# Backward chain of a recurrent-memory attention layer: the left queries' part of the key gradient packed by row and head, its rows in three scratch tensors, another issue order

## The chip, the cores and the metric

The kernel runs on one core of one Trainium2 chip. The metric is the device time of one execution in microseconds. A core has TensorE (PE; its weight loads are shown as PEld), VectorE (DVE), ScalarE (ACT), GpSimd (POOL), SyncE (SP), and sixteen DMA engines that SP and POOL issue to.

## The reference, cut to what matters

The forward function normalises x [2048, 512], adds a recurrent attention (A) and a dense layer with squared ReLU (B); what must be computed is its output and the gradients of all ten inputs. The attention runs over 64 segments of 32 rows, one after the other, each with 8 memory rows that come from the segment before:

```python
for s in range(n_seg):
    xs = x[:, s * seg_len:(s + 1) * seg_len, :].copy()
    h = jnp.concatenate([mem, xs], axis=1)             # 8 + 32 rows
    q = jnp.einsum('btd,dhe->bhte', h, Wq)             # 32 heads of 128; k and v alike
    ...
    scores = jnp.where(mask[None, None], scores, -1000000000.0)
    p = _softmax(scores, axis=-1)
    o = jnp.einsum('bhqk,bhke->bhqe', p, v)
    o = jnp.einsum('bhte,hed->btd', o, Wo)
    mem = o[:, :M, :].copy()
    outs.append(o[:, M:, :])
...
_out, _vjp = jax.vjp(_f, A_x, A_mem0, A_Wq, A_Wk, A_Wv, A_Wo, B_w1, B_b1, B_w2, B_b2)
_grads = _vjp(grad_out)
```

The gradient with respect to the memory rows of a segment is needed by the segment before, so the backward pass is a chain of 64 steps too. This case's change is in the gradient with respect to the keys: for each head, the transposed gradient of the scores times the queries, summed over all 40 query rows of a segment.

## The kernel before

The program has five stages: the dense layer and its gradient (to about 290 us); the forward chain (to 1155 us); the left stage, the part of the backward pass that does not depend on the chain (to 1384 us); the backward chain (1384 to about 2318 us); and the weight gradients of the attention (to the end).

**Rows.** The 40 rows of a segment are split. The 32 rows "memory and 24 tokens" are the main rows; the remaining 8 rows of each of four segments are gathered to 32 "left" rows of a block. A block b is four segments (SPB = 4), there are NB = 16 blocks. The 32 heads are four groups (HG = 4) of eight (KH = 8); the group g takes partitions 32g to 32g+31, so one array pass serves four groups side by side. KK is 4, M is 8, L is 40, KW is 64, GW is 1024 (eight heads of 128).

**Left queries in the chain.** A step's key gradient has two parts: from the main queries qN (32 rows) and their score gradients gS, and from the left queries qNL (32 rows of the block, of which 8 belong to the step) and their score gradients GL, which the left stage has computed and stored in S_GSL. In kp (half p of the heads, four heads each) both parts go through outer, which issues for each of four heads and each part four products, one per row group: 16 products from qN with 40 columns and 16 from qNL with 16 columns, which add to the same PSUM:

```python
def kp(p=p):
    outer(pp(p), p, ((KW, L, False, 32, C["qN"], lambda k: gS[:, k, 0:L]),
                     (KW, KW, True, 32, B_["qNL"], pair)))
```

The products from qNL contract all 32 left rows of the block with the columns of GL that belong to the step.

**Scratch.** Left query, key and value rows are computed in the forward part, evicted (L401 and E_ of the forward chain) and stored in one tensor S_NL with three places per row. turned_rows and left_of_step read them back.

**Order.** In the backward chain nothing is planned at run time: B_ORDER lists the operations of four steps, one string for each of the four steps of a block, and play calls them in that order; each engine keeps its own instructions in the order of the calls, and waits for others by semaphores. A name with four plus signs belongs to the step that starts in this string; "L." marks work of a block. The names used here:

- o0mm, o1mm: projection of the output gradient (ps_proj); o0fl, o1fl, o0te, o1te: its transposes and their copies
- vp, kp, qp with half 0 or 1: outer products for v, k and q gradients (b_pp), into one pair of PSUM double banks that all share; ve, vl, ke, kl, qe: their evictions on ACT and DVE, to gv, gk, gq and to b_gvL and b_gkL
- s, d1 to d4, tu: score gradients on TensorE and DVE, and their transposition
- vg, kg, qg: products with the weights (ps_gR, ps_R); ra, rb, ta, tb, Ha, Hb: sum, transposition and reduction to the gradient that the next step starts from
- ldp, ldq, ldn, ldk, vtr, pb, vc: loads of a step and their copies; ldk loads kLs, four loads of 8 rows
- L.G0 to L.I3: left products of the block before (ps_RL); L.vo, L.ko, L.qo (two each): stores of the block's gradients to S_GB; L.lq: the load of gqL; L.ldk: GL and qNL of the next block, on POOL's queue; L.vtr, ktr, qtr and vst, kst, qst: transposes of left gradients and their stores to S_GL

gv, gk and gq have one buffer each, so a block's first evictions wait for the stores of the block before. The loads of qNL, GL, kLs, qN, kN have one buffer, P has two. SP issues the loads of ldk and vtr, all stores and the transposes; POOL issues ldp, ldq, ldn and L.ldv.

## Time and profile before

| what | value |
|---|---|
| median of 3 runs (lowest, highest) | 2909.87 us (2907.95, 2930.09) |
| the profiled execution, its own time | 2896.93 us |
| its span on the core | 2894.9 us |
| granted TensorE clock, mean | 0.978 |
| PE, PEld, DVE, ACT, POOL busy | 94%, 51%, 45%, 36%, 23% |
| DMA: bytes, mean rate | 561.55 MB, 194 GB/s |
| packets under 512 B, of 792984 | 583601 |

Busy time of an engine is the union of its instructions' spans; a matmul's span includes its way through the array, so several products in four row groups overlap. The chain that ended last is 79% on PE and 9% on DMA by the page.

### The profile page before, as it was taken

To read this page: it belongs to the slowest core of one execution; us is meant where nothing else is said; L and a number is where in the kernel's file an instruction comes from. 1 tells how busy PE (TensorE), PEld (TensorE's weight loads), DVE (VectorE), ACT (ScalarE), POOL (GpSimd) and SP (SyncE) were. 2 spreads that over 40 slices of the span, in tenths; PEclk is the share of its full clock that TensorE was granted. 3 is DMA by queue.
4 is the path that set the end of the run, shared out by engine and by line. 5 is a ranking of instruction groups with operands and counts; after the bars stand their busy time and mean duration, and the time that the engine had idled before them with its cause. 6 is when DMAs were issued, how large, how long until landed. Compare 5 with 4: busy or idle time off the path is not lost.

```text
span 2894.9 us, 116348 instructions
## 1 busy us (share of the span) xinstructions
PE 2713.6 (94%) x51700; PEld 1472.0 (51%) x51700; DVE 1298.9 (45%) x3786; ACT 1029.3 (36%) x2362; POOL 658.1 (23%) x1279
## 2 busy tenths in 40 slices
PE   7998899999999888889899999999999889999999
PEld 3554555555555555547455545554555434444444
DVE  5552566666666555444445544554555401100000
ACT  2422445444445444433333333333333301111111
POOL 1000000000000000113333433343344333322221
PEclk9999999999999999999999999999999999999999
DMA  9649377776776666998666787778677799999992
GB/s 262 225 122 239 97 183 189 184 187 182 193 184 179 169 166 161 258 249 247 162 166 173 186 216 177 178 194 208 174 185 193 231 270 221 204 209 248 205 213 68
DMA packets 792984, 561.55 MB, mean 194 GB/s; under 512 B 583601, under 2 KB 683458, under 8 KB 789154
## 3 DMA queue, kind: packets, MB, share of 16 engines
q1 hardware_dynamic: 751426, 430.34, 63.5%
q0 software_dynamic: 41056, 123.77, 14.0%
q8 instruction: 405, 6.64, 0.9%
q14 instruction: 97, 0.79, 0.1%
HBM read 189.15 MB, written 234.11 MB: 146 GB/s over the span
## 4 chain that ended last, share of the span: by engine, by line
PE 79%; DMA 9%; DVE 5%; SPq 3%; issue 3%; ACT 2%; POOL 0%; ACTq 0%; DVEq 0%; POOLq 0%
PE ps_gw L1643 16%; PE ps_proj L428 15%; PE ps_gR L496 11%; PE ps_R L496 5%; PE b_pp L626 3%; PE ps_tr L165 3%; PE ps_L L388 3%; PE ps_RL L1255 3%; DMA b_kLs<-S_NL 2%; PE ps_w L1110 2%; PE ps_sc L473 2%; PE f_pp L626 2%; PE ps_B L340 2%; PE f_T L531 2%; PE b_T L531 2%
## 5 line engine op out<-in xcount | busy, mean ns | idle before, releaser
L1643 PE MATMUL ps_gw<-gn,HNc 128*128 128x512 bf16 x1920 | 418.7, 380 | 2.1 <-DMA gn<-S_GL 2.1
L1643 PEld LDWEIGHTS <-HNc 128*128 128x128 bf16 x1920 | 188.2, 98 | 227.3 <-issue 5.0
L410 ACT CAST f_N<-ps_proj 128x512 bf16<-128x512 f32 x320 | 183.6, 580 | 197.7 <-PE ps_proj L428 189.9
L1576 ACT CAST wt<-ps_gw 128x512 bf16<-128x512 f32 x128 | 74.1, 587 | 454.1 <-PE ps_gw L1643 413.9
L428 PEld LDWEIGHTS <-X 128*32 128x32 bf16 x6144 | 154.3, 96 | 143.6 <-DVE X L540 22.2
L1559 DVE TENSOR_TENSOR gx<-ps_rows,gb 128x512 f32<-128x512 f32 x16 | 11.1, 692 | 431.9 <-PE ps_rows L1557 431.9
L901 POOL COPY kM<-f_kT 128x256 bf16<-128x256 bf16 x64 | 25.6, 401 | 736.7 <-DVE f_kT L413 562.7
L1643 PE MATMUL ps_gw<-GOc,gn 128*128 128x512 bf16 x640 | 141.6, 384 | 8.4 <-ACT wt L1576 6.9
L496 PE MATMUL ps_gR<-Wv,gv 128*32 128x512 bf16 x2048 | 144.5, 403 | 2.5 <-issue 2.3
L496 PE MATMUL ps_gR<-Wk,gk 128*32 128x512 bf16 (+1 forms) x2048 | 139.3, 387 | 1.9 <-issue 0.9
L428 PE MATMUL ps_proj<-Wq,X 128*32 128x512 bf16 x2048 | 134.9, 380 | 2.2 <-issue 2.1
L410 ACT CAST gk<-b_pp 128x256 bf16<-128x256 f32 x192 | 70.7, 379 | 178.4 <-PE b_pp L626 114.2
L496 PE MATMUL ps_R<-Wo,OT 128*32 128x256 bf16 x4096 | 132.9, 286 | 1.1 <-DVE OT L413 1.1
L428 PE MATMUL ps_proj<-Wk,X 128*32 128x512 bf16 x2048 | 132.7, 383 | 0.6
L410 ACT CAST gON<-ps_proj 128x512 bf16<-128x512 f32 x128 | 74.9, 585 | 156.5 <-PE ps_proj L428 156.5
L428 PE MATMUL ps_proj<-Wv,X 128*32 128x512 bf16 x2048 | 129.5, 378 | 0.0
L428 PE MATMUL ps_proj<-Wo,GT 128*32 128x512 bf16 x2048 | 123.7, 382 | 4.2 <-DVE GT L1300 3.5
L1577 POOL DMA_DIRECT2D out_dram<-wt x120 | 64.8, 542 | 268.6 <-ACT wt L1576 253.5
L496 PE MATMUL ps_gR<-Wq,gq 128*32 128x512 bf16 (+1 forms) x2048 | 118.2, 343 | 1.6 <-issue 1.5
L1336 POOL COPY PD<-b_P 32x320 bf16<-32x320 bf16 x256 | 114.7, 448 | 8.0
L496 PEld LDWEIGHTS <-OT 128*32 128x32 bf16 x4096 | 108.1, 101 | 9.2 <-DVE OT L413 1.3
L1331 POOL DMA_DIRECT2D b_P<-S_A x63 | 33.8, 537 | 343.0 <-DVE gS L585 105.0
(283 smaller groups left out, 5346.0 us busy)
## 6 DMA issues: line engine op xcount, KB each, us to landing
S_A<-f_N SPq DMA_DIRECT2D x64, 512.0 KB
out_dram<-wt POOLq DMA_DIRECT2D x134, 128.0 KB, 5.2
S_A<-f_N SPq DMA_DIRECT2D x64, 256.0 KB
S_GB<-gv SPq DMA_DIRECT2D x32, 512.0 KB
S_GB<-gq SPq DMA_DIRECT2D x32, 512.0 KB
S_GB<-gk SPq DMA_DIRECT2D x32, 512.0 KB
b_kN<-S_A POOLq DMA_DIRECT2D x63, 256.0 KB, 3.8
b_qN<-S_A POOLq DMA_DIRECT2D x63, 256.0 KB, 3.8
```

The lines of the kernel that those rows point to most:

```text
L165: nc.tensor.transpose(ps_ap, in_ap, ident[base:base + k, base:base + k])
L388: nc.tensor.matmul(ps[:], lhsT=x(dc), rhs=Wqkv[t][:, dc, c0:c0 + 512], start=(dc == 0), stop=(dc == DC - 1))
L410: nc.scalar.copy(out, in_)
L428: nc.tensor.matmul(o, lhsT=hT[:, dc, :], rhs=x, start=(dc == 0), stop=(dc == DC - 1), tile_position=(0, 32 * g))
L496: nc.tensor.matmul(R[32 * g:32 * g + 32, 0:(cs.stop - cs.start) * P].rearrange("p (a b) -> p a b", b=P), lhsT=XT(k, g), rhs=x[:, cs, :], s ...
L531: nc.tensor.transpose(st["T", h][:, 0, c * P:(c + 1) * P], st["R4"][:, (2 * h + c) * P:(2 * h + c + 1) * P], identF[:])
L626: nc.tensor.matmul(o, lhsT=N_[32 * g:32 * g + m, kk * P:(kk + 1) * P], rhs=X(kk)[32 * g:32 * g + m], start=(i == 0), stop=(i == len(jobs) ...
L1255: nc.tensor.matmul(ps["R", i][32 * g:32 * g + 32, :].rearrange("p (a b) -> p a b", b=P), lhsT=B_[n][:, k, g, :], rhs=W(g * KH + k), start= ...
L1336: nc.gpsimd.tensor_copy(PD[32 * g:32 * g + 32, g], C["P"][32 * g:32 * g + 32, :, 0:L])
L1576: nc.scalar.copy(wt[:], ps[:])
L1577: eng(dst, wt[:])
L1643: nc.tensor.matmul(ps[:], lhsT=l(rc), rhs=r(rc), start=(n == 0), stop=(n == RC_ALL - 1))
```

## The change

The left queries' part of kp becomes four products per half step, one per row group. To that end 8 rows of the step and 4 heads are put on the 32 partitions of a group: qNL is now loaded as [row and head, step, half, 128], and the score gradients are brought to block-diagonal form, so that a partition of one head is zero in the columns of the three others. The left stage sums the score gradients over the steps' places (of which all but one are zero, c0 and c1 on DVE) to gC and stores it in S_GC; ldg loads it by heads, and gx on POOL multiplies it by the one-hot matrix ofk to GX. S_NL becomes three tensors, and the left query rows are stored with the head order changed, for which left_out and the scores of the left rows take care. ldk and the new ldg are four loads each on SP's queue, in place of two on POOL's. LB_ORDER gets c0 and c1, B_ORDER is another order throughout.

The diff, without context where it isn't needed; the calls of outer lose one argument in the other stages, and left_out, the left scores and the loads by S_NL[t] are used alike in the forward part:

```diff
-    S_NL = dram.tile([NB, P, 3, GW], BF16, name="S_NL")
+    S_NL = [dram.tile([NB, P, GW], BF16, name="S_NL%d" % t) for t in range(3)]
-    S_GSL = dram.tile([NB, P, KH, KW], BF16, name="S_GSL")
+    S_GC = dram.tile([NB, P, KK, 4 * M], BF16, name="S_GC")
...
+    ofk = const.tile([P, KK], BF16, name="ofk")
+    with nc.allow_low_precision(reason="all terms of a sum but one are zero"):
+        nc.vector.tensor_reduce(ofk[:], ident[:].rearrange("p (a k) -> p k a", k=KK), axis=AX.X, op=ALU.add)
...
         for dc in range(DC):
             nc.tensor.matmul(ps[:], lhsT=x(dc), rhs=Wqkv[t][:, dc, c0:c0 + 512], start=(dc == 0), stop=(dc == DC - 1))
+    def left_out(cp, dN, ps, t, h):
+
+        if t:
+            cp(dN[:, h * 512:(h + 1) * 512], ps[:])
+        else:
+            cp(dN[:].rearrange("p (k h e) -> p h k e", k=KK, h=2)[:, h], ps[:].rearrange("p (k e) -> p k e", k=KK))
+
     def keep_left(dN, q, t, g):
-        dma(S_NL[4 * q:4 * q + 4, 32 * g:32 * g + 32, t, :].rearrange("b r c -> r b c"), dN[:])
+        dma(S_NL[t][4 * q:4 * q + 4, 32 * g:32 * g + 32, :].rearrange("b r c -> r b c"), dN[:])
     with sb("fl", 2) as fl:
         dma(XL1[:], S_XL[:])
         dma(Wo[:], A_Wo.rearrange("h e d -> e h d"))
...
-                    nc.tensor.matmul(sc3[32 * g:32 * g + 32, k, c:c + n], lhsT=qT[:, 4 * h + k, g, :],
+                    nc.tensor.matmul(sc3[32 * g:32 * g + 32, k, c:c + n], lhsT=qT[:, head(h, k), g, :],
...
         for nm, f in (("mx", mxf), ("sb", sbf), ("ex", exf), ("su", suf), ("rc", rcf), ("pm", pmf)):
             o["%s%d" % (nm, p)] = f
-    def outer(pp, h, jobs, base=0):
+    def outer(pp, h, jobs, base=0, first=True):
         for k in range(4):
-            for i, (c0, w, ends, m, N_, X) in enumerate(jobs):
+            for i, (c0, w, m, N_, X) in enumerate(jobs):
                 for g in range(HG):
                     o = pp[g // 2][:, g % 2, base + k * c0:base + k * c0 + w]
-                    if ends:
-                        o = o.rearrange("p (a n) -> p a n", a=2)[:, :, 0:M]
                     kk = 4 * h + k
                     nc.tensor.matmul(o, lhsT=N_[32 * g:32 * g + m, kk * P:(kk + 1) * P],
-                                     rhs=X(kk)[32 * g:32 * g + m], start=(i == 0), stop=(i == len(jobs) - 1),
+                                     rhs=X(kk)[32 * g:32 * g + m], start=(first and i == 0), stop=(i == len(jobs) - 1),
                                      tile_position=(32 * g, 0), skip_group_check=True)
     def two_of(pp, x, w, base=0, n=4):
...
-                "d10 d20 d30 d40 so- x0- tu0 W0b d11 d21 d31 d41 tu1 v0 x1-").split()
+                "d10 d20 d30 d40 so- x0- tu0 W0b d11 d21 d31 d41 tu1 c0 c1 v0 x1-").split()
...
                     turn(st[p], T["gS"], p)
                 o["tu%d" % p] = tu
+                def own(p=p):
+                    with nc.allow_low_precision(reason="all terms of a sum but one are zero"):
+                        nc.vector.tensor_reduce(
+                            T["gC"][:, :, p].rearrange("p k (a t) -> p k a t", a=2),
+                            T["gS"][:, HALF[p]].rearrange("p k (a j t) -> p k a t j", a=2, j=SPB), axis=AX.X, op=ALU.add)
+                o["c%d" % p] = own
+
                 def qp(p=p):
                     ps["x", p] = [lpp.tile([P, 2, 512], F32, name="l_pp", tag="pp%d" % x) for x in range(2)]
-                    outer(ps["x", p], p, ((32, 32, False, 32, T["kM"], lambda k: st[p][:, k % 4, 0, :]),
-                                          (32, 32, False, 32, T["kL"], lambda k: st[p][:, k % 4, 1, :])))
+                    outer(ps["x", p], p, ((32, 32, 32, T["kM"], lambda k: st[p][:, k % 4, 0, :]),
+                                          (32, 32, 32, T["kL"], lambda k: st[p][:, k % 4, 1, :])))
                 o["qp%d" % p] = qp
                 for x, n in enumerate("ab"):
                     o["qe%s%d" % (n, p)] = lambda p=p, x=x: acp(
...
-        "o0mm++++ pb+++ o1mm++++ L.vo1+ L.qst o0ev++++ L.vo0+ xa+++ L.xt L.qo0+ o1ev++++ o0fl++++ xb+++ L.ra0+ "
-        "vp0++++ o0te++++ L.G2+ vea++++ s0++++ d10++++ o1fl++++ d20++++ ldp++++ d30++++ ldq+++ vla++++ o1te++++ "
-        "vp1++++ ldn+++ ldp+++++ L.I1+ L.G1+ vlb++++ d40++++ veb++++ L.ko0+ s1++++ d11++++ L.ko1+ ldk+++ kp0++++ "
-        "vg1++++ tu0++++ L.qo1+ keb0++++ d21++++ qp0++++ kla0++++ vg0++++ kea0++++ d31++++ qeb0++++ d41++++ "
-        "kg0++++ klb0++++ vtr++++ tu1++++ qp1++++ ldn++++ L.sx+ qeb1++++ qea0++++ qg0++++ qea1++++ kp1++++ "
-        "qg1++++ keb1++++ kea1++++ kg1++++ vc++++ klb1++++ kla1++++ ra++++ pb++++ rb++++ ldq++++ L.H2+ ta++++ "
-        "tb++++ Ha++++ Hb++++",
-        "o0mm++++ o0ev++++ o1mm++++ o1ev++++ xb+++ o0fl++++ vp0++++ xa+++ o0te++++ vla++++ s0++++ o1fl++++ "
-        "vp1++++ d10++++ vea++++ d20++++ L.H1+ o1te++++ ldk+++ L.ktr+ d30++++ d40++++ veb++++ vlb++++ tu0++++ "
-        "vtr++++ vtr+++++ s1++++ d11++++ d21++++ d31++++ vg0++++ kp0++++ qp0++++ d41++++ vg1++++ qea0++++ "
-        "qeb0++++ qg0++++ keb0++++ tu1++++ L.kst+ kla0++++ klb0++++ kp1++++ kea0++++ kea1++++ kg0++++ qp1++++ "
-        "keb1++++ kla1++++ ldk++++ qeb1++++ L.ra1+ L.I2+ kg1++++ qea1++++ L.ra2+ qg1++++ klb1++++ ra++++ L.G3+ "
-        "rb++++ ta++++ L.vtr+ ldp+++++ Ha++++ tb++++ Hb++++",
-        "o0mm++++ ldq+++ xb+++ o1mm++++ o0ev++++ o0fl++++ vc+++ xa+++ o1ev++++ pb+++ o0te++++ vp0++++ s0++++ "
-        "d10++++ vea++++ d20++++ o1fl++++ vp1++++ o1te++++ vg0++++ vla++++ ldn+++ s1++++ d30++++ d40++++ d11++++ "
-        "veb++++ tu0++++ d21++++ vlb++++ kp0++++ keb0++++ vg1++++ d31++++ L.sl d41++++ qp0++++ tu1++++ L.vst+ "
-        "L.gs+ kea0++++ qea0++++ klb0++++ kla0++++ L.I3+ kg0++++ qeb0++++ kp1++++ qp1++++ qea1++++ kea1++++ "
-        "keb1++++ qeb1++++ qg0++++ klb1++++ kla1++++ L.gl++ L.gst+ kg1++++ qg1++++ ra++++ L.H3+ ta++++ rb++++ Ha++++ "
-        "tb++++ ldp+++++ Hb++++",
-        "o0mm++++ o1mm++++ L.ldt++ o0ev++++ ldq+++ ldn+++ vc+++ L.ra3+ xb+++ o1ev++++ xa+++ vtr++++ o0fl++++ "
-        "pb+++ vp0++++ vc++++ o1fl++++ o0te++++ s0++++ ldk+++ vea++++ vla++++ o1te++++ d10++++ d20++++ vp1++++ "
-        "s1++++ d30++++ veb++++ vlb++++ d40++++ d11++++ vg0++++ kp0++++ L.tb+ kla0++++ tu0++++ d21++++ qp0++++ "
-        "vg1++++ d31++++ keb0++++ d41++++ kea0++++ kg0++++ kp1++++ qeb0++++ tu1++++ L.G0++ klb0++++ qp1++++ L.ta+ "
-        "qea0++++ L.qtr+ qg0++++ L.lq++ L.ldv++ qeb1++++ kea1++++ keb1++++ qea1++++ kg1++++ klb1++++ qg1++++ "
-        "L.I0++ ra++++ rb++++ ta++++ kla1++++ tb++++ L.H0++ Ha++++ Hb++++ L.ldk++")
+        "L.lq+ Hb+++ o0mm++++ o1mm++++ o0ev++++ o0fl++++ vp0++++ L.ra3 o1ev++++ xa+++ o0te++++ L.ta xb+++ ldp++++ "
+        "vea++++ vtr++++ s0++++ o1fl++++ d10++++ d20++++ vla++++ L.tb d30++++ o1te++++ vp1++++ d40++++ L.G0+ L.I1+ "
+        "tu0++++ ldq+++ s1++++ L.gs+ L.vst+ d11++++ kp0++++ vlb++++ d21++++ d31++++ ldn+++ d41++++ veb++++ qp0++++ "
+        "L.sx+ tu1++++ L.I0+ kea0++++ ldq++++ L.xt qea0++++ L.H0+ vg1++++ ldn++++ keb0++++ qeb0++++ vg0++++ kla0++++ "
+        "kg0++++ L.ra0+ kp1++++ qp1++++ klb0++++ qg0++++ kla1++++ qea1++++ keb1++++ qeb1++++ qg1++++ kea1++++ "
+        "klb1++++ kg1++++ ldp+++++ pb++++ ldk++++",
+        "ra+++ rb+++ L.G1+ ta+++ L.sl Ha+++ vc+++ tb+++ Hb+++ xa+++ L.qtr+ o0mm++++ o1mm++++ vtr++++ o0ev++++ "
+        "o1ev++++ L.H1+ o0fl++++ xb+++ vp0++++ o0te++++ o1fl++++ s0++++ vc++++ vla++++ o1te++++ d10++++ vea++++ "
+        "vp1++++ ldq++++ s1++++ d20++++ d30++++ d40++++ ldk++++ vtr+++++ tu0++++ vg0++++ kp0++++ d11++++ vlb++++ "
+        "veb++++ qp0++++ d21++++ keb0++++ d31++++ d41++++ klb0++++ vg1++++ pb++++ qea0++++ tu1++++ qeb0++++ qg0++++ "
+        "kp1++++ kea1++++ ldn++++ kla0++++ kea0++++ kla1++++ qp1++++ klb1++++ qea1++++ kg0++++ keb1++++ qeb1++++ "
+        "L.ra1+ kg1++++ qg1++++ ra++++ L.G2+ rb++++ vc+++++ ta++++",
+        "Ha+++ tb+++ Hb+++ o0mm++++ o1mm++++ xa+++ o0ev++++ o0fl++++ xb+++ o0te++++ vp0++++ s0++++ d10++++ L.H2+ "
+        "o1ev++++ d20++++ d30++++ vp1++++ vea++++ L.ldg++ veb++++ o1fl++++ vla++++ vg0++++ L.ldt++ d40++++ tu0++++ "
+        "o1te++++ kp0++++ qp0++++ ldp++++ vlb++++ vg1++++ keb0++++ s1++++ kla0++++ kea0++++ ldn++++ L.gst+ qea0++++ "
+        "L.qst+ klb0++++ d11++++ d21++++ qeb0++++ kg0++++ d31++++ d41++++ qg0++++ kp1++++ L.I2+ keb1++++ kla1++++ "
+        "tu1++++ kea1++++ qp1++++ kg1++++ qea1++++ qeb1++++ klb1++++ L.ra2+ qg1++++ ra++++ ldp+++++ L.G3+ ldk++++ "
+        "ta++++ vtr+++++ rb++++ Ha++++ L.gl++ tb++++ Hb++++",
+        "o0mm++++ ldq+++ o0ev++++ o1mm++++ pb+++ xb+++ vp0++++ o1ev++++ vea++++ o0fl++++ o1fl++++ xa+++ vp1++++ "
+        "o0te++++ o1te++++ s0++++ veb++++ L.vo0++ vlb++++ vla++++ s1++++ d10++++ d20++++ d30++++ d40++++ vg0++++ "
+        "vg1++++ tu0++++ d11++++ kp0++++ kea0++++ klb0++++ qp0++++ d21++++ d31++++ L.I3+ keb0++++ d41++++ pb++++ "
+        "L.vo1++ qea0++++ tu1++++ kg0++++ kp1++++ L.ko0++ kla0++++ qeb0++++ qg0++++ qp1++++ klb1++++ kea1++++ "
+        "kla1++++ qeb1++++ keb1++++ kg1++++ L.ktr++ qea1++++ L.ldk++ vc++++ qg1++++ L.ldv++ L.ko1++ L.H3+ L.kst++ "
+        "ra++++ L.gx++ ta++++ ldk++++ rb++++ L.qo0++ L.qo1++ L.vtr++ tb++++ Ha++++")
...
-                          "gqL": (bt, [P, KH, HG, NL], BF16), "GL": (be, [P, 1, KH, KW], BF16),
-                          "gOL": (be, [P, GW], BF16), "qNL": (be, [P, GW], BF16), "vTL": (be, [P, KH, HG, NL], BF16),
+                          "gqL": (bt, [P, KH, HG, NL], BF16), "GC": (bt, [P, SPB, 2, 2 * M], BF16),
+                          "GX": (be, [P, SPB, 2, KK, 2 * M], BF16),
+                          "gOL": (be, [P, GW], BF16), "qNL": (be, [P, SPB, 2, P], BF16), "vTL": (be, [P, KH, HG, NL], BF16),
-                    return pool.tile(shape, dt, name="b_" + n, tag=n)
+                    return pool.tile(shape, dt, name="b_" + n, tag="XL" if n == "GC" else n)
...
                 q(PGD[32 * g:32 * g + 32, g], S_PL[b][32 * g:32 * g + 32])
             q(block(b)["gOL"][:], S_GOL[b])
-        def ldk(b, q=pdma):
-            q(block(b)["GL"][:, 0], S_GSL[b])
-            q(block(b)["qNL"][:], S_NL[b][:, 0, :])
+        def ldk(b, q=dma):
+            by_heads(q, block(b)["qNL"], S_NL[0][b].rearrange("r (k c) -> r k c", k=KK))
+
+        def ldg(b, q=dma):
+            by_heads(q, block(b)["GC"], S_GC[b])
+
+        def by_heads(q, dst, src):
+
+            for g in range(HG):
+                r = slice(32 * g, 32 * g + 32)
+                q(dst[r].rearrange("p j h c -> p j (h c)"), src[r].rearrange("(j t) k c -> (t k) j c", j=SPB))
+
+        def gx(b):
+            shape = [P, SPB * 2, KK, 2 * M]
+            nc.gpsimd.tensor_tensor(
+                out=block(b)["GX"][:].rearrange("p j h k c -> p (j h) k c"),
+                in0=block(b)["GC"][:].rearrange("p j h c -> p (j h) c").unsqueeze(2).to_broadcast(shape),
+                in1=ofk[:].unsqueeze(1).unsqueeze(3).to_broadcast(shape), op=ALU.mult)
         def ldt(b):
             turned_rows(block(b)["vTL"][:], b, 2)
-        loads.update(gl=gl, ldv=ldv, ldk=ldk, ldt=ldt)
+        loads.update(gl=gl, ldv=ldv, ldk=ldk, ldt=ldt, ldg=ldg, gx=gx)
         def bwd(s):
             b, j = divmod(s, SPB)
...
-                def pair(k):
-
-                    return B_["GL"][:, 0, k, :].rearrange("p (a n) -> p a n", a=2)[:, :, lc]
-
...
                                          start=False, stop=True, skip_group_check=True)
                 def kp(p=p):
-                    outer(pp(p), p, ((KW, L, False, 32, C["qN"], lambda k: gS[:, k, 0:L]),
-                                     (KW, KW, True, 32, B_["qNL"], pair)))
+                    x = pp(p)
+                    for g in range(HG):
+                        r = slice(32 * g, 32 * g + 32)
+                        nc.tensor.matmul(
+                            x[g // 2][:, g % 2, 0:4 * KW].rearrange("p (k a n) -> p k a n", k=KK, a=2)[:, :, :, 0:M],
+                            lhsT=B_["qNL"][r, j, p, :], rhs=B_["GX"][r, j, p].rearrange("p k (a n) -> p k a n", a=2),
+                            start=True, stop=False, tile_position=(32 * g, 0), skip_group_check=True)
+                    outer(x, p, ((KW, L, 32, C["qN"], lambda k: gS[:, k, 0:L]),), first=False)
                 def qp(p=p):
-                    outer(pp(p), p, ((32, 32, False, 32, C["kN"], lambda k: st[p][:, k % 4, 0, :]),
-                                     (32, 32, False, M, C["kLs"], lambda k: st[p][:, k % 4, 1, :])), 4 * KW)
+                    outer(pp(p), p, ((32, 32, 32, C["kN"], lambda k: st[p][:, k % 4, 0, :]),
+                                     (32, 32, M, C["kLs"], lambda k: st[p][:, k % 4, 1, :])), 4 * KW)
                 o["vp%d" % p], o["kp%d" % p], o["qp%d" % p] = vp, kp, qp
                 def v_half(p=p):
                     return pp("v")[p][:].rearrange("p c (k g n) -> p g (c k) n", k=2, g=HG)
...
+            ldg(NB - 1)
+            gx(NB - 1)
```

## The prediction

> **What bounds the kernel now.** I read the page first, then the busy time by stretch, then the waits of TensorE in the backward chain, and last the timelines of single steps. The page and one stretch of the backward chain (1384 to 2305 us, 64 steps in 16 blocks of four):
>
> ```profile
> PE 2713.6 (94%) x51700; PEld 1472.0 (51%) x51700; DVE 1298.9 (45%) x3786; ACT 1029.3 (36%) x2362; POOL 658.1 (23%) x1279
> ...
> 1800.00:2100.00 300.00, 282.33 (x7496) 154.28 (x7491) 152.46 (x477) 117.44 (x321) 118.05 (x232) 0.99 0.74 186
> ```
>
> The columns of the second line are the window, its length, busy time of PE, PEld, DVE, ACT and POOL with instruction counts, granted clock, DMA share and GB/s. TensorE sets the end, and in the chain 18 us of 300 are still idle, at a clock of 0.99 and a DMA share of 0.74. So there are two things to win: TensorE work, and its waits. Steps begin with the 32 products of ps_proj:
>
> ```profile
> 1802.68 1.91 PE L428 MATMUL ps_proj<-Wo,GT 128*32 128x512 bf16 x32
> ...
> 1815.74 1.91 PE L428 MATMUL ps_proj<-Wo,GT 128*32 128x512 bf16 x32
> ```
>
> That was a second step of a block: 13.06 us. Over all blocks but the first, the steps last on the mean (smallest): first 16.85 (15.41), second 13.17 (13.06), third 12.95 (12.73), fourth 14.83 (14.22). Second and third steps are at their floor and repeat it to 0.01 us. They carry three and two groups of left products (ps_RL, 0.44 us each); the first carries four, so its floor is 13.06 + 0.44 = 13.5, and it loses 3.35 us per block; the fourth loses 0.6. Together 64 us over 16 blocks. What the first step waits for:
>
> ```profile
> 1851.49 0.37 ACT L410 CAST gk<-b_pp 128x256 bf16<-128x256 f32 x1 [2.73 <-DMA S_GB<-gk]
> ...
> 1840.18 2.62 SPq L1242 DMA_DIRECT2D S_GB<-gk  x2
> 1842.84 5.13 SPq L645 DMA_DIRECT2D b_kLs<-S_NL  x4
> 1848.07 0.55 SPq L1242 DMA_DIRECT2D S_GB<-gq  x1
> ```
>
> Columns: start, duration, engine, line, what; in brackets the idle time before and its releaser. The step began at 1843.25. The key gradients of the last block are issued for storing at 1840.2 to 1842.8 and have landed at 1851.5, some 8.7 us later; until then ScalarE may not write the new block's gk into the same buffer, and TensorE stands behind it. The small loads of kLs (x4) take 5.13 us to issue there, 0.3 us each elsewhere. So the store of three gradients, 3 MB in one burst at the block's end, is what the first step pays for. The waits of TensorE over the chain carry other names as well:
>
> ```profile
> PE b_pp L626 <- issue: 19.0, 16, 3.3
> PE b_pp L626 <- DVE gS L585: 9.0, 12, 1.0
> PE b_pp L626 <- DMA b_kLs<-S_NL: 5.7, 9, 1.4
> ```
>
> (total, times, longest.) "issue" is time without a releaser in the profile; it falls into the same first and fourth steps.
>
> **The change, part by part.**
>
> *Products.* kp has now 32 products per half step: four heads times four row groups from qN (40 columns), and the same from qNL (16 columns). The 16 of qNL become 4 of 64 columns; 12 per half step go, 12 x 128 = 1536 in all, with as many weight loads. Their price is seen in a burst without gaps:
>
> ```profile
> 1820.60 0.20 PE L626 MATMUL b_pp<-gS,b_qN 32*128 32x40 bf16 x4
> 1820.62 0.19 PE L626 MATMUL b_pp<-b_GL,b_qNL 32*128 32x16 bf16 x4
> 1820.65 0.20 PE L626 MATMUL b_pp<-gS,b_qN 32*128 32x40 bf16 x4
> 1820.68 0.19 PE L626 MATMUL b_pp<-b_GL,b_qNL 32*128 32x16 bf16 x4
> 1820.70 0.20 PE L626 MATMUL b_pp<-gS,b_qN 32*128 32x40 bf16 x4
> ```
>
> The 0.19 us of one product is its latency; a group of four starts every 0.026 us, with 40 columns or 16. A group of 64 columns is put at 0.027 (a 512-column ps_gw takes 34.53 / 160 = 0.216 us, so 64 columns 0.027). Three groups fewer: 3 x 0.026 x 128 = 10 us less. Bounds: nothing saved if the packed group costs as much as four (0.10 us), 13 us if it is free. I take -10. The Trainium skill, TensorE: Matmul & The Clock Gate, section Back-to-back issue gap, has a much dearer pair of weight load and product, 81 ns at 128 columns in a sustained stream; at that price, as an estimate, 12 x 81 ns x 128 = 124 us would go. Here 32 pairs in four row groups take 0.21 us, 6.6 ns each, and the trace decides.
>
> *Work added.* In the left stage DVE gets 32 reductions of 256 elements to 64; the nearest row is ds_r at 128x256, 420 ns, so 0.84 us per block. DVE is busy 45% there and TensorE sets the stage; hidden, at worst 16 x 0.84 = 13 us. POOL gets 16 products of 128x512 (gx); the nearest rows are its tensor_tensor of 128x512 at 1152 ns. POOL is busy 118 of 300 us and loses two DMA issues of 0.54 us per block, so the balance is nothing. But gx must wait for kp1 of the fourth step and for its load, and behind it on POOL stand pb, ldp, ldq, ldn of the next step; their loads run a step ahead (b_kN lands 3.8 us after its issue). No cost; if that cover went, one wait of about 1 us per block, 16 us.
>
> *Loads moved from POOL's queue to SP's.* Two issues per block become eight on SP, at about 0.35 us: 2.8 us of SP per 57 us block. They stand in the third and fourth step ahead of the last key store, the kLs loads and the query stores. The bytes are the old ones, so the DMA share hardly moves. At the chain's start they stand ahead of the first kp0: +3 us (8 x 0.35). At its end the load of gqL now follows the last stores instead of preceding them; the last block's products need it: +2 us, bounds 0 and 8.7 (the landing above).
>
> *Left rows in three tensors.* The same rows of 2 KB; the query rows are written with their heads in another order and the scores pick them so. The copies keep their size (128x512). Nothing, both ways.
>
> *The stores earlier.* In the new order the value stores go out in the middle of the fourth step, as soon as its values are evicted, and the key and query stores follow inside that step; before, all were listed in the next block's first step. The burst then begins some 6 us sooner, and the first eviction of gk, 5 to 6 us into the first step, finds it landed. Of the 64 us I take 9/10 away: -58. Bounds: 0 (the stores merely collide elsewhere) and -64.
>
> *New waits.* The new order puts evictions between two products of one pair of PSUM banks, with no TensorE work to cover them. In the second step kp1 is followed on TensorE directly by qp1, while kea1 (DVE) and a b_gkL copy (ACT) are listed between and read the same banks. Rows for this, of a third step:
>
> ```profile
> 1938.48 0.42 DVE L413 CAST gk<-b_pp 128x256 bf16<-128x256 f32 x1 [2.09 <-ACT gq L410]
> 1938.93 0.21 ACT L410 CAST b_gkL<-b_pp 128x64 bf16<-128x64 f32 x1 [0.22 <-DVE gk L413]
> ```
>
> The copy on ACT begins 0.03 us after DVE's ended: the two go one behind the other. So qp1 waits 0.17 (end of kp1) + 0.42 + 0.21 + 0.05 = 0.85 us. Before, kg0 (0.98 us) stood between. By the same count: qg0 of the second step behind a DVE copy listed after d21, d31, d41 (0.35 us each) 0.5; qp1 of the third, partly covered by I2, 0.65; of the fourth, qp0 behind kea0 0.55 and kg1 directly behind qp1 and two copies per engine 1.3; qg1 of the first 0.4. Sum 4.25 us per block. Copies that follow each other on one engine overlap by 0.1 (1936.15 and 1936.41 on ACT: 0.26 apart, 0.38 long), so about 3.4: 16 x 3.4 = +54. Bounds: 0, if other waits hold TensorE up anyway at these places, and 4.25 x 16 = 68.
>
> *Sum.* -10 - 58 + 54 + 3 + 2 = -9 us. The profiled execution took 2896.9 us (span 2894.9), so 2888; the runs' median is 2909.9, 0.45% more, hence 2901 for it.
>
> **The rivals.**
>
> *The burst goes and the new waits don't come* (chance 0.26). TensorE would need to find its banks free, as in the second and third steps now, whose order leaves 0.12 us of gaps. Against it are the rows above: the copies do go one behind the other. -10 - 64 + 10 + 5 = -59: 2851.
>
> *The burst only moves, and the waits come* (0.22; the slower side). The stores share SP with eight more loads, and each waits for room on its queue: the kLs loads' 5.13 us show that SP gets stuck when the burst is out. In the new order kst, which waits for a transpose, and four kLs loads stand between the key and the query stores. If the last key store is issued later than about 3 us before the block's end, 8.7 us of landing bring it past the first gk eviction, and the first step keeps most of its loss. With two thirds kept, -21 in place of -58, and waits of 60: -10 - 21 + 60 + 5 = +34: 2944. For it: DMA share 0.74, full in the burst. Against: the value stores, a third of the bytes, are then out before.
>
> *The packing gives nothing* (0.04): a packed group as dear as four, then +1: 2911.
>
> *Pairs at the price of the skill's stream* (0.01): -124 in place of -10: 2787. The 6.6 ns speak against it.
>
> **How the numbers follow.** The forecast has 0.47: about 2901, its own range 2880 to 2925 from the bounds of the moved load, the packing and a third of the waits either way. One per cent, 29 us, is about what a measurement of this kernel can tell from no change. From the forecast come 0.41 within, 0.03 on either side; the first rival gives 0.25 to faster and 0.01 within; the second 0.21 to slower and 0.01 within; the third 0.03 within and 0.01 slower; the last 0.01 faster. Faster 0.29, within 1% 0.46, slower 0.25. The range reaches below the first rival's value and above the second's by the 13 us that bound the reductions and the packing: 2838 to 2957.
>
> **What would show it.** Products: 512 of 64 columns, kp bursts of about 0.13 us in place of 0.21. Stores: no ACT wait on S_GB<-gk, first steps near 14.5 us. New waits: second steps about 13.8, fourth steps losing about 1.5 us to evictions, on rows of b_pp and ps_gR released by gk. If second and third steps stay at 13.06 and 12.73 less the packing, the first rival holds; if first steps stay above 16 with gk waiting on S_GB, the second. I am wrong if the change of the time comes from outside 1384 to 2320 us.

## The result, and the profile after

The changed kernel takes 2953.71 us (median; 2950.09 to 2966.45) against 2908.91 us: a ratio of 1.0139, 95% interval 1.0105 to 1.0174, 45 us slower. The forecast was 2901 with 2838 to 2957 as its range. The profiled execution took 2950.09 us (span 2948.3).

The page of the kernel after, and the same stretch of its chain by busy time:

```profile
PE 2705.5 (92%) x50164; PEld 1469.6 (50%) x50164; DVE 1327.0 (45%) x3819; ACT 1030.3 (35%) x2362; POOL 664.7 (23%) x1265
```
```profile
1800.00:2100.00 300.00, 265.53 (x6492) 145.55 (x6496) 145.90 (x444) 110.22 (x299) 108.62 (x205) 0.98 0.76 174
```

TensorE has 1536 products fewer and 8 us less to do, and yet stands twice as long: 34 us of 300 where it was 18. The DMA share rose from 0.74 to 0.76 though fewer steps fell into the stretch. Beginnings of a second and a third step (timeline of TensorE):

```profile
1947.55 1.91 PE L438 MATMUL ps_proj<-Wo,GT 128*32 128x512 bf16 x32
...
1961.28 1.91 PE L438 MATMUL ps_proj<-Wo,GT 128*32 128x512 bf16 x32
```

13.73 us from one to the next, the shortest second step of all; before, 13.06 came back again and again. By place in the block, mean of 15 blocks: first 18.96 us (16.85 before), second 14.45 (13.17), third 13.28 (12.95), fourth 14.53 (14.83). The 53.4 us by which the span grew are, from the steps' starts: chain +52.8 (first steps, the first block's too, +33.1, second +20.2, third +5.0 with one left group more, fourth -5.6 with one less), its start -3.7, its end +17.8, the weight stage -13.4 (TensorE stood 9.1 us in it before and lost 5.1 to the clock; now it does not stand and loses 0.5). The kp burst is as forecast, four packed products and then sixteen:

```profile
1980.01 0.21 PE L1424 MATMUL b_pp<-b_GX,b_qNL 32*128 32x64 bf16 x4
1980.05 0.26 PE L634 MATMUL b_pp<-gS,b_qN 32*128 32x40 bf16 x16
```

The waits of TensorE in the chain (total us, times, longest):

```profile
PE b_pp L634 <- DMA b_kLs<-S_NL: 22.7, 16, 2.9
PE b_pp L634 <- ACT b_gkL L420: 12.0, 15, 0.8
PE ps_gR L506 <- DVE gk L423: 11.6, 15, 0.8
PE b_pp L1424 <- DMA b_qNL<-S_NL: 8.9, 11, 2.3
PE b_pp L634 <- DVE gk L423: 8.8, 15, 1.1
PE b_pp L634 <- ACT gk L420: 7.5, 15, 0.5
PE ps_gR L506 <- ACT gk L420: 6.6, 17, 0.4
```

Two kinds: loads of left rows (kLs, qNL), about once per block and long, and copies out of PSUM, 15 times each and short. ScalarE's wait for S_GB<-gk, on which the forecast rested, is gone; it waits for S_GB<-gq now, and SP for a transpose. The first line is of before, the others are of after:

```profile
ACT gk L410 <- DMA S_GB<-gk: 19.1, 9, 2.7
ACT gq L420 <- DMA S_GB<-gq: 12.9, 14, 2.2
SPq L1302 <- DMA gNat<-b_gkL: 48.3, 15, 6.5
```

What a first step waits for now (timeline; the step began at 1927.45):

```profile
1923.89 1.69 SPq L1293 DMA_TRANSPOSE gNat<-b_gkL  x1
...
1925.68 2.02 SPq L1332 DMA_DIRECT2D b_qNL<-S_NL  x4
...
1927.80 0.56 SPq L1257 DMA_DIRECT2D S_GB<-gk  x1
...
1932.27 0.35 SPq L1302 DMA_DIRECT2D S_GL<-gNat  x1
1932.71 1.30 SPq L653 DMA_DIRECT2D b_kLs<-S_NL  x4
...
1936.64 0.82 PE L634 MATMUL b_pp<-gST,b_kLs 8*128 8x32 bf16 x4 [2.89 <-DMA b_kLs<-S_NL]
```

SP stood from 1928.4 to 1932.3 for the transpose of the left key gradient; the key rows listed behind its store landed 3.9 us after their issue, and TensorE stood 2.89 us in qp0. What that does to its clock is in the stretches of 3 us around it (columns as in the prediction):

```profile
1930.00:1933.00 3.00, 2.79 (x68) 1.83 (x65) 2.67 (x9) 1.51 (x4) 0.00 (x0) 1.00 0.97 221
1933.00:1936.00 3.00, 0.71 (x23) 0.39 (x23) 2.19 (x9) 0.00 (x0) 0.00 (x0) 1.00 0.68 240
1936.00:1939.00 3.00, 2.32 (x44) 1.15 (x48) 0.05 (x1) 1.32 (x5) 0.00 (x0) 0.67 1.09 365
1939.00:1942.00 3.00, 3.00 (x48) 1.18 (x40) 0.18 (x1) 0.62 (x2) 0.00 (x0) 0.76 1.07 146
1942.00:1945.00 3.00, 2.79 (x94) 1.28 (x90) 0.89 (x3) 0.76 (x3) 1.81 (x4) 1.00 1.21 333
```

The granted clock is 0.67 and 0.76 for the 6 us after the stand: 1.7 us more lost. The last column but one shows the DMA engines at 0.97 to 1.21 of their time (packets overlap) in four of the five stretches, and at 0.68 in the one in which TensorE stands. Taken by half steps, as means over 14 blocks, that share is:

| kernel | fourth step, halves | first step, halves | second step, halves | third step, halves |
|---|---|---|---|---|
| before | 0.79, 0.88 | 1.09, 0.77 | 0.42, 0.50 | 0.64, 0.70 |
| after | 1.03, 0.91 | 0.98, 1.09 | 0.62, 0.28 | 0.37, 0.59 |
| e7 | 1.02, 0.71 | 1.10, 1.06 | 0.58, 0.32 | 0.40, 0.61 |
| e13 | 1.05, 0.73 | 1.07, 0.72 | 0.58, 0.57 | 0.64, 0.57 |

### The profile page after: what moved, and what is told of

Same layout as the page of the kernel before. It is cut to its first block, busy times and chain, and to the rows that moved or that the text cites. A ratio compares the mean times of both kernels' runs of the same rounds, so it can differ in the third digit from the quotient of the medians.

```text
span 2948.3 us, 113428 instructions
## 1 busy us (share of the span) xinstructions
PE 2705.5 (92%) x50164; PEld 1469.6 (50%) x50164; DVE 1327.0 (45%) x3819; ACT 1030.3 (35%) x2362; POOL 664.7 (23%) x1265
## 4 chain that ended last, share of the span: by engine, by line
PE 76%; DMA 10%; DVE 7%; ACT 3%; issue 2%; SPq 2%; POOL 0%; ACTq 0%; DVEq 0%; POOLq 0%
PE ps_gw L1677 19%; PE ps_proj L438 14%; PE ps_gR L506 9%; PE ps_R L506 4%; DMA gNat<-b_gkL 3%; PE ps_L L391 3%; PE ps_tr L168 3%; PE b_pp L634 2%; PE ps_RL L1270 2%; PE ps_w L1125 2%; PE ps_w L1120 2%; PE ps_sc L483 2%; PE f_pp L634 2%; PE f_T L541 1%; PE ps_B L343 1%
## 5 line engine op out<-in xcount | busy, mean ns | idle before, releaser
L506 PE MATMUL ps_gR<-Wq,gq 128*32 128x512 bf16 (+1 forms) x2048 | 126.9, 342 | 10.3 <-ACT gq L420 4.2
L1379 POOL COPY b_vT<-b_vl 128x1024 bf16<-128x1024 bf16 x64 | 66.9, 1045 | 205.1 <-PE ps_sc L483 151.2
```

The costliest lines, as they stand in the source:

```text
L506: nc.tensor.matmul(R[32 * g:32 * g + 32, 0:(cs.stop - cs.start) * P].rearrange("p (a b) -> p a b", b=P), lhsT=XT(k, g), rhs=x[:, cs, :], s ...
L1379: nc.gpsimd.tensor_copy(vT[:, :, :, 0:SEG], C["vl"][:])
```

## The experiments

Four theories, named so in the expectations. A: the new issue order costs the time, by the place of single operations in a queue and by copies left uncovered. B: the packing's data path costs it. C: SP's queue passes its lateness on, so that a repaired place only makes the next transfer late. D: the DMA engines are full around a block's start, and what is last there is late. Each time stands against runs of the kernel before on the same chip, and differences below are between these distances; after stands at +44.8 us. (The expectations of e7 and its followers take bare medians, which give 24 and 26 us where I have 20 and 22.)

| run | us | before | ratio, 95% interval | first, second, third, fourth step, mean us |
|---|---|---|---|---|
| e1 | 2927.2 | 2905.2 | 1.0079, 1.0054 to 1.0105 | 17.80, 12.93, 12.54, 16.33 |
| e2 | 2949.9 | 2905.2 | 1.0153, 1.0115 to 1.0191 | 17.89, 14.42, 13.49, 15.44 |
| e3 | 2929.9 | 2905.2 | 1.0082, 1.0053 to 1.0111 | 15.49, 16.42, 13.29, 14.60 |
| e4 | 2928.1 | 2905.2 | 1.0086, 1.0056 to 1.0116 | 19.56, 13.58, 13.30, 13.39 |
| e5 | 2936.3 | 2908.6 | 1.0090, 1.0059 to 1.0122 | 18.98, 14.37, 13.26, 14.51 |
| e7 | 2903.0 | 2908.6 | 0.9981, 0.9958 to 1.0003 | 18.52, 13.21, 13.29, 13.31 |
| e8 | 2932.9 | 2908.6 | 1.0083, 1.0055 to 1.0112 | 18.78, 12.91, 12.53, 15.53 |
| e9 | 2920.5 | 2908.6 | 1.0039, 1.0009 to 1.0068 | 17.91, 13.11, 13.01, 15.50 |
| e10 | 2973.7 | 2904.4 | 1.0251, 1.0220 to 1.0283 | 17.08, 13.49, 13.39, 18.78 |
| e11 | 2958.5 | 2904.4 | 1.0190, 1.0160 to 1.0220 | 19.98, 13.12, 13.12, 15.20 |
| e12 | 2989.6 | 2904.4 | 1.0304, 1.0267 to 1.0341 | 20.78, 13.52, 13.64, 16.26 |
| e13 | 2887.0 | 2904.5 | 0.9952, 0.9931 to 0.9973 | 16.50, 13.53, 13.36, 14.03 |
| e14 | 2897.2 | 2904.5 | 0.9984, 0.9957 to 1.0012 | 17.45, 12.91, 12.49, 15.38 |
| e15 | 2952.2 | 2904.5 | 1.0179, 1.0144 to 1.0214 | 19.39, 13.48, 13.76, 14.59 |
| e16 | 2935.3 | 2903.7 | 1.0112, 1.0055 to 1.0169 | 18.77, 12.94, 12.48, 15.52 |
| e17 | 2884.6 | 2903.7 | 0.9929, 0.9903 to 0.9955 | 15.76, 13.49, 13.53, 14.72 |

**The two halves of the change.** e1 is the changed kernel with the four strings of before; e2 the kernel before with the four strings of after.

```diff
 e1, third string:  ... kg1++++ ... L.H3+ ...
+                   L.ldg++            (ahead of L.gl++)
 e1, fourth string: ... L.I0++ ra++++
+                   L.gx++
 e2: B_ORDER of after
-                   L.ldg++ L.gx++
```

> Packed products, by-head loads, sums and broadcast as in the changed kernel, but the four strings of the backward order are those of before, with only the load of the packed score gradients and the broadcast added. If the issue order is what costs (theory A): each burst of left products is 0.215 - 0.143 = 0.07 us shorter, times 128 is 9 us, less up to 5 us for eight more transfers on SP per block: 2900 to 2910 us. If the new data path costs (theory B: by-head loads on SP, broadcast on GpSimd, 32 sums on VectorE): 2930 to 2955 us.

> The products, loads and scratch of before, but the four strings of the backward order of the changed kernel, without the two new operations. Theory A (order): as slow as the changed kernel plus the 9 us of the longer bursts, less some us for eight SP transfers per block that are gone: 2945 to 2965 us, with first steps of a block near 18 to 19 us. Theory B (data path): 2905 to 2920 us, first steps near 16 us.

e1 is 22 us slower than before, between the theories; e2 is 45 us slower, as A said. So the order costs 45 us without the packing too, and the packing, which should have gained, costs 22 in the old order. In e1 the second and third steps did fall, to 12.93 and 12.54 us; the first and fourth rose. The main waits of TensorE in e1 and in e2:

```profile
PE b_pp L634 <- DMA b_kLs<-S_NL: 28.9, 30, 2.7
...
PE b_pp L1368 <- DMA b_gOL<-S_GOL: 20.2, 10, 2.6
```

With the old products the new order loses by another load: in e2 TensorE waits 0.4 us for kLs, where after has 22.7, and 20.2 for gOL, which stands on GpSimd's queue behind the two long loads that only the old products have. That both come to 45 us is in part chance. In the kernel before TensorE waits 5.7 us for kLs; in e1 eight more loads stand on SP ahead of the key rows and of the stores.

**Single places of the new order.** e3, e4 and e5 each undo one thing in the changed kernel.

```diff
 e3, fourth string
+ ldk++++ L.ktr++ ... L.kst++ ra++++ L.gx++ ta++++
- ldk++++ rb++++ ...
 e4, second string
- kp1++++ kea1++++ ldn++++ kla0++++ kea0++++ kla1++++ qp1++++ klb1++++ qea1++++ kg0++++ keb1++++ qeb1++++
+ kp1++++ kea1++++ ldn++++ kla0++++ kea0++++ keb1++++ kla1++++ kg0++++ qp1++++ klb1++++ qea1++++ qeb1++++
 e4, fourth string
- kp0++++ kea0++++ klb0++++ qp0++++
+ kp0++++ qp0++++ kea0++++ klb0++++
- qeb0++++ qg0++++ qp1++++ klb1++++ kea1++++ kla1++++ qeb1++++ keb1++++ kg1++++
+ qeb0++++ kea1++++ keb1++++ qg0++++ qp1++++ klb1++++ kla1++++ qeb1++++ kg1++++
- qg1++++ L.ldv++ L.ko1++ L.H3+
+ L.H3+ qg1++++ L.ldv++ L.ko1++
 e5: L.lq+ at the head of the first string
- L.lq+
+ L.lq++ ahead of L.kst++ in the fourth string
```

> The changed kernel with one name moved in the last string: the load of the next step's left key rows (four transfers on SP) is issued ahead of the transpose of the left key gradient and its store, so that it no longer queues behind them. If that load makes the first steps long (mean 18.96 us): the 2.9 us stand at the second query product goes, and with it the slow stretch after it, 2 to 2.5 us; times 15 steps is 65 to 80 us: 2875 to 2900 us, and first steps of 14.5 to 15.5 us. If another item takes its place in SP's queue (the store of the left key gradient or the next loads, now later): 2930 to 2955 us, first steps above 17 us.

> The changed kernel with TensorE work put between a product and the copies that the next product waits for, in the second and fourth step of a block (key-gradient gather ahead of the second query product, query product straight after the key product, left group ahead of the last gather). By the waits counted after the change: 0.9 + 0.6 us in the second step, 0.57 + 1.0 + 0.6 in the fourth, 3.7 us per block, 55 us over 15 blocks: 2895 to 2915 us if all of it goes, and steps of about 12 us (second) and 12.5 us (fourth). If the copies themselves set the pace (ScalarE and VectorE late, the wait only moves to the next product): 2940 to 2955 us.

> The changed kernel with the load of the left query gradient (b_gqL) put back into the last string of the order, ahead of the left key store and not behind the next block's start. The end of the backward chain stands 12.2 us for this load; from the last step's start to the first product of the weight stage it takes 46.1 us where it took 28.3 us before. If the place of this load is the whole of it: that stretch falls to 28 to 32 us and the time to 2936 to 2942 us. If the load, waiting on SP for its buffer, holds up the left key store and the next left key rows: first steps rise from a mean of 19.0 us to 20 us or more and the time is 2950 to 2965 us.

e3: first steps fell by 3.5 us, nearly to what A said, and second steps rose by 2.0. The first line below is TensorE's wait, the second GpSimd's ahead of it:

```profile
PE b_pp L1393 <- DVE b_XT L550: 29.4, 15, 3.9
...
POOL b_XT L1463 <- DMA S_XG<-b_XT: 47.9, 15, 4.8
```

The store of b_XT, next in SP's queue, was now late; GpSimd could not clear the tile, VectorE could not write it, and the next vp0 stood. 20 us of the expected 65 to 80 remain. e4: 22 us faster; second and fourth steps fell by 0.9 and 1.1 us, but first steps rose by 0.6, of which the longer waits for kLs and qNL (25.0 and 11.0 us in all, 22.7 and 8.9 in the kernel after) are some 0.3. Not half of the forecast gain. e5: 17 us faster by the medians, at the edge of what the two intervals tell apart. The stretch at the chain's end fell from 46.1 to 39.9 us, which shows 6 of them. The profiled execution was the slowest of e5's five, 2949.5 us, and tells nothing of the rest.

**All repairs together, and the same move in the old order.** e7 has e3, e4, e5 and two more places; e8 and e9 bring the key rows of the first step forward in the old order, with and without the packing.

```diff
 e7 = e3 + e4 + e5, and
- L.sx+ (after qp0++++)      + xb+++ L.sx+        first string
- L.ldk++ (after L.ktr++)    + L.ldk++ L.ko0++    fourth string
 e8 (from e1), e9 (from before), first string
+ ldk+++ o0mm++++ ...
- L.ko1+ ldk+++ kp0++++
+ L.ko1+ kp0++++
 e8, fourth string
+ ldk+++ L.ldg++             (and not in the third string)
```

> The changed kernel with four edits of its order together: left key rows ahead of the left key transpose (run alone 24 us faster, its second steps 2 us longer because VectorE's b_XT waited for the store of S_XG), TensorE work over the new waits (run alone 26 us faster), the left query gradient's load in the last string, and now also the store of S_XG issued as soon as its rows are there, ahead of the other transposes, and the left query rows ahead of the first key store. If order on SP and the uncovered copies are the whole loss (theory A): first steps 15.5 us, second 13.6, third 13.3, fourth 13.4, sum 55.8 against 61.2 us per block; times 16 is 86 us, with 15 us at the end: 2850 to 2870 us. If the queue only passes its lateness on to the next item (theory C: SP has too much to issue around the start of a block): first and second steps together stay above 31 us and the time is 2890 to 2915 us.

> Packing in the order of before (run alone 22 us slower than before), with the left key rows of the first step issued ahead of the six stores of the block, and the four loads of the packed score gradients after the fourth step's key rows and not ahead of them. In that run TensorE waits 28.9 us for b_kLs, 30 times, all in first and fourth steps; after each such stand it runs slowly for a while. Theory A (queue order): first steps 15 to 15.5 us for 17.8, fourth 14 for 16.3, times 15 is 65 to 75 us: 2855 to 2870 us. Theory C (the queue passes its lateness on): the copies of gk wait for the stores, as in the kernel before; first steps stay at 17 us, 2895 to 2920 us.

> The kernel before with the one move in the first string: the left key rows of the first step ahead of the block's stores; products as before. It tells how much of the gain in the packed variant of the same move is the move and not the packing. In before, TensorE waits 5.7 us for b_kLs and its stores are the ones that hold ScalarE. Theory A: with no eight extra loads on SP the rows were hardly late, so 5 to 15 us: 2890 to 2900 us. Theory C: the stores go out later by the 2 us of four loads, and the copies of gk stand longer: 2905 to 2920 us.

e7 takes back the whole loss, 2903 us, but in the way of C: first and second steps together are 31.7 us, and first steps alone 18.5. On SP the last store of gq stood behind the transpose of the left key gradient and its store. The second line is TensorE behind ScalarE, the first ScalarE behind the last store:

```profile
ACT gq L420 <- DMA S_GB<-gq: 69.4, 15, 5.1
...
PE ps_gR L506 <- ACT gk L420: 38.7, 17, 3.3
```

e8 is slower than both theories said, e9 is 12 us slower than before, at the upper end of C. In e8 the rows' wait fell from 28.9 to 13.0 us, and TensorE waited 46.1 us for copies of b_gvL, behind copies of gv that waited 64.5 us for S_GB<-gv. Theory A, a few wrong places, falls: one place repaired delays another.

**Are the DMA engines full?** e11 adds bytes to the kernel before; e10 takes transfers away from the block's start, e12 does that with the old products.

```diff
 e11, so() of before, for n == "v"
+ dma(S_GB2[b][:, gs, ks], G4[n][:, gs, ks].rearrange("p g k j r -> p g k (j r)"))
 e10 = e7, and
- L.gs+ L.vst+ (first string)  L.qtr+ (second)  L.ktr++ L.kst++ L.vtr++ (fourth)
+ ldk++++ L.gs+ L.ktr+ ... kp1++++ L.kst+ L.vtr+        second string
+ o1mm++++ L.vst+ L.qtr+ ...                            third string
 e12: before with the order of e10, without L.ldg++ and L.gx++
```

> The kernel before, and the value gradient of each block is stored a second time, into a scratch tensor that nothing reads: two more transfers of 512 KB on SP next to the six of S_GB. Theory D: 1 MB at the 347 GB/s of the first half of a first step is 3 us, and as the DMA engines are full there the first step grows by it: 16 times 3 is 48 us, 2940 to 2960 us. Theory A (SP's issue alone): two issues of 0.5 us, 16 us at most, 2908 to 2925 us. If the copies of gk and gq stand for something else, no change, 2900 to 2912 us.

> The order of e7 (four repairs of the changed kernel's order) with six more operations moved: the three transposes of left gradients, their stores S_GL and the transpose for b_GN go from around the start of a block into its second and third step. In the changed kernel the DMA engines are busy 0.98 to 1.09 of the first step and 1.03 of the first half of the fourth, but 0.28 to 0.37 from the middle of the second to the middle of the third. Theory D (the transfers around a block's start fill the DMA engines, and whichever is issued last is late): these transfers, some 1.5 MB with three stores of 256 KB, are 4 to 6 us of all engines; first steps fall from 18.5 us to 14.5 to 15.5 us, 15 times 3 to 4 us is 45 to 60 us off 2903: 2845 to 2860 us, and the share in the first step falls below 0.9. Theory A (a single name in SP's order, which e7 has put right): first steps stay at 18 us or more, 2895 to 2910 us. The store of S_GB is then still waited for by the copies of gq or gk.

> The products, loads and scratch of before in the order of e10. Against e10 it says what the packing itself is worth once the order is not in its way. By the bursts 0.215 against 0.143 us, times 128: e10 faster by 9 us. By the DMA engines: packing adds by head 512 packets of 64 B and 512 of 512 B per block where before there were 256 long ones; if their share counts, e10 loses 1 to 2 us per block, 15 to 30 us, and e12 is the faster. Both 2845 to 2875 us if spreading the left stores works, both near 2900 us if not.

e11 came out as D said: 54 us slower, first steps 3.1 us longer; the share in their first half is 1.05 at 363 GB/s. About 1.65 of the 3.1 us are the clock, which fell in the second half from 0.893 to 0.745: 10.0 x 0.255 - 8.4 x 0.107. D had no such term, so the 3 us that it gave came out in part by luck. The delay is seen at SP: two more issues, and the last kLs load went out 6.4 us into the first step and not 3.3; a store of gk, once issued, released the copy after 8.7 us, 9.0 before. e10 missed all it was given, though its first steps fell by 1.4 us and the share of their second half from 1.06 to 0.75. The chain of transposes and stores, which share one buffer, now stood on SP ahead of the fourth step's key rows:

```profile
PE b_pp L634 <- DMA b_kLs<-S_NL: 48.6, 13, 6.2
```

e12 missed both of its values too, at 2990 us: TensorE waited 48.4 us for gOL, behind the long loads on GpSimd's queue.

**Spread, but not ahead of a load that is due.** e13 starts that chain at the head of the second step; e15 is its order with the old products; e14 is e1 with the left query rows on GpSimd's queue.

```diff
 e13 = e7, with the same names taken out as in e10, and in the second string
+ vtr++++ L.gs+ L.ktr+ L.kst+ L.vtr+ L.vst+ o0ev++++ ... ldk++++ L.qtr+ ... kp1++++ L.qst+
 third string
- L.qst+
 e14 (from e1)
- def ldk(b, q=dma):
+ def ldk(b, q=pdma):
 e15: before with the order of e13, without L.ldg++ and L.gx++
```

> As e10, but the chain of left transposes and their stores, which share one buffer and take 3.7 us each way, starts 11 us earlier, at the start of the second step, where SP and the DMA engines are nearly idle (0.21 to 0.25), and so ends before the fourth step's key rows have to go out. In e10 those rows stood behind it and TensorE waited 48.6 us for them in fourth steps, while first steps fell from 18.5 to 17.1 us. Theory D (DMA engines full around a block's start; the rest is place in the queue): fourth steps back at 13.3 us, first 15.5 to 17, second 13.5, third 13.3: 55.6 to 57.1 us per block against 58.2 of e7, 2865 to 2890 us. If the lateness moves on to another transfer again (theory C): one of the four places above by 3 us or more, 2900 to 2930 us.

> Packing in the order of before (2927 us), but the four loads of the left query rows go out on GpSimd's queue, where the two loads of before were, and not on SP ahead of the block's stores. Theory A (place in SP's queue): the stores go out 2.8 us earlier per block, first and fourth steps return to the 16.9 and 14.8 us of before, second and third keep the 0.2 and 0.4 us that the shorter bursts gave them: 2895 to 2905 us. Theory D (what the transfers take of the DMA engines, 512 packets of 512 B for 128 long ones, and 512 of 64 B): the queue does not matter, 2918 to 2930 us.

> The products and loads of before in the order of e13. Against e13 it gives the worth of the packing where the order does not stand against it. In the order of e10 the packed products were 16 us faster than the old ones, 1 us per block, more than the 0.6 us by which the bursts are shorter. If the worth is the bursts alone: e15 slower than e13 by 9 us; if it also has to do with what GpSimd issues (its two long loads of 256 and 128 KB at a block's end, which are gone): by 15 to 30 us.

e13: 2887 us, as D said, and faster than the kernel before by 0.5%, the interval below 1. First steps have 16.5 us and fourth 14.0, where D had 13.3; the DMA engines are full for one half of the first step and not for both. From after to e13 only the order is changed, and it is worth 62 us. But e13 does not tell D from a place in SP's queue, for the moved transpose and store stood ahead of the stores of gq. By the timelines (means of 15 blocks) the last store of gq went out 7.0 us into the first step in e7 and 3.3 in e13, and from its issue to the release of the copy it took 4.1 us in e7 and 5.3 in e13. It was issued sooner, not carried faster. ScalarE's wait, 69.4 us in e7, became

```profile
ACT gq L420 <- DMA S_GB<-gq: 28.7, 15, 3.7
```

e14: 2897 us, as A said, though first and fourth steps came only part of the way back, to 17.45 and 15.38 us: the same transfers from the other queue are worth 29 us against e1. The Trainium skill, DMA: Bandwidth & Descriptors, section Issuing engines are not separate DMA queues, says that issuing from several engines saves only the time to initiate; here more hung on what stands behind those issues, and the measurement decides. e15 is 65 us slower than e13, far more than the bursts: the two long loads on GpSimd's queue now stood ahead of gOL, for which TensorE waited:

```profile
PE b_pp L1368 <- DMA b_gOL<-S_GOL: 39.6, 13, 5.0
```

So the packing's worth hangs on the order and the queue: -22 us in the old one (e1) and 7 with the other queue (e14, not to be told from nothing), nothing in the new one (e2 against after), 16 in that of e10, 65 in that of e13. How much of the 16 and of the 65 is the packing and how much the queue of its loads was not taken apart.

**What is left.** e16 moves loads on GpSimd's queue in e14, e17 moves 256 KB out of the block's start in e13.

```diff
 e16 (from e14)
- ... Hb++++ L.ldk++ (fourth string)     + kp1++++ L.ldk++
- ldq+++ vla++++ (first string)          + ldq+++ o0mm++++ pb+++
 e17 (from e13)
- L.ko1++ L.lq++ (fourth string)         + L.lq+ ra+++ (head of the second string)
```

> As e14 (packing, order of before, left query rows on GpSimd's queue; 2897 us), and on that queue the four loads of the left query rows go out right after their last reader in the fourth step and not at its end, and the query rows of the first step (b_qN) ahead of GpSimd's copies for that step and not behind them. In e14 TensorE waits 32.2 us for b_qN, 14 times, in fourth and first steps. Theory A (place in a queue): two thirds of it go, with the slow stretch behind each stand: first steps from 17.5 to 15.5 to 16.5 us, 2868 to 2885 us. Theory D (the DMA engines, 1.12 busy in the first half of a first step, make whatever is last late): it moves to b_kLs or to the store of S_GB, 2890 to 2905 us.

> As e13 (2887 us), with the load of the left query gradient, 256 KB, moved from the block's end to the start of the next block's second step. Theory D: 256 KB at 341 GB/s are 0.77 us less in the first step and no store stands behind it on SP: 10 to 15 us less in the chain, 2870 to 2880 us, if the end of the chain, where this load then comes after the last stores, does not give it back (40.3 us from the last step's start to the first product of the weight stage in e13, at most 12 us more: 2885 us). Theory A: a load that nobody in the first step waits for does not matter, 2884 to 2900 us.

e16 is slower than e14 by 39 us, against both: b_qN is no longer waited for, but gOL and a copy behind it are.

```profile
PE b_pp L1395 <- DMA b_gOL<-S_GOL: 21.3, 13, 2.6
PE b_pp L1393 <- POOL PD L1346: 18.0, 15, 2.5
```

e17's first steps fell by 0.74 us, the 0.77 that D said for 256 KB, but fourth steps rose by 0.7 and the end of the chain from 40.3 to 46.5 us. In all 2884.6 us, 0.7% faster than before, and not to be told from e13.

## Why the prediction was wrong

**Products, -10: right.** From first issue to last a burst went from 0.200 to 0.129 us (medians), 0.07 x 128 = 9 us. e1's second and third steps are 0.24 and 0.41 us shorter, more than the 0.14 of two bursts; where the rest comes from is open.

**Work added: right.** Nothing waits for the reductions, and GpSimd's broadcast is waited for once, at the chain's start.

**New waits, +54: right.** TensorE's waits for copies of gk, b_gkL and gq (seven rows, 53.2 us, five of them above) stood at 4.9 before, so +48. In e4 16.9 us of them were left, and 22 us were won. Second steps grew by 1.28 us; the count before its cut for overlap, less 0.16 for the bursts, gives 0.85 + 0.5 - 0.16 = 1.19.

**The stores earlier, -58: the step that failed.** The sum had the key and query stores inside the fourth step, some 6 us sooner, and the first step's loss gone with the wait for them. By the timelines (means of 15 blocks, from the first step's start, minus is ahead of it) only half of that came: the last value store went out at -9.9 us in place of -6.1 and the first key store at -7.2 in place of -3.9, but the last key store at +0.4 in place of -2.3, and the two query stores at 6.3 and 6.8 in place of -4.8 and 4.3. What an order lists is not what SP issues: the old stores were listed in the first step and mostly out before it, and in the new order SP stood for its transposes, 3.2 us per block for that of the left key gradient alone. The copies of gk no longer wait for S_GB, as I said, but not for the reason given: the store they waited for left later, and they themselves begin at 9.1 us, not 7.3.

The loss stayed, in a first step 2.1 us longer where the sum had it 2.8 shorter (-3.0 of the 58, +0.3 of the waits, -0.16 of the bursts): 4.9 us x 16 = 78 us. With 17 less for fourth steps that came out better and 5 more for second ones that is the miss in the chain, +52.8 against a forecast of -14. In place of the stores TensorE waits for the kLs loads (22.7 us), the last of which went out at 5.9 us in place of 3.3, behind the transpose and its store. e3 shows it: with these loads ahead of the transpose first steps fell from 18.96 to 15.49 us. That second steps then grew by 2.0 us for another store on SP, and that first steps are back at 18.5 us in e7, where the last stores of gq stand behind the transpose, shows that the loss belonged not to one store but to what stands on SP around a block's start.

Whether the DMA engines, full around a block's start (theory D), are a cause of it in this kernel is not shown. For it speaks e11, where 1 MB more put SP's later issues back by 3 us. Against it: in after the four kLs loads of a first step take about 1.3 us to issue, where before they took 4.9 on the mean; e3's first steps are the shortest but their DMA share is 1.11 and 1.13 in the two halves; e12 and e15 have 0.37 and 0.38 in the second half and first steps of 20.8 and 19.4 us; and e13's gain over e7 goes with an earlier issue. How much of its 12 us are the bytes and how much the place on SP, no run separates. One row of the prediction told that SP is slow at a block's start, and I read it singly: the 5.13 us that four small loads took to issue. I put more onto that queue and gave it no price in the steady state.

**Loads on SP, nothing in the steady state: mis-sized.** e1 against e14 puts the place of the four query-row loads ahead of the stores and key rows at 29 us in the old order.

**The slower rival** (2944, chance 0.22) had the size and the items in the queue, kst and four kLs loads. Its condition came too, the last key store later than 3 us before the block's end. It had the wrong victim: not the copies behind that store, but the kLs loads themselves.

**The clock** was no term of the sum. In first steps' second halves it was 0.893 before and 0.875 after, in their first 0.991 and 0.943: 9.45 x (0.125 + 0.057) = 1.7 us against 1.0, so 0.7 of the 2.1 us.

**Start +3, end +2.** The chain began 3.7 us earlier. Its end took 17.8 us longer, the weight stage 13.4 less, +4.4 together, within the bounds; the load of gqL was waited for 12.2 us.
